# Weight scaling taken off GpSimd, small squares moved to ScalarE, and a new written-out order in a fused attention and MoE kernel

## The chip, the cores and the metric

The kernel runs on one core of one Trainium2 chip. The core has five queues of work that matter here: TensorE (PE; its weight loads are listed as PEld), VectorE (DVE), ScalarE (ACT), GpSimd (POOL), and SyncE (SP), whose queue issues all the DMAs of this kernel. The metric is the device time of one execution in microseconds; lower is better.

## The reference

Three layers follow each other over 2304 tokens (4 batches of 576), in float32:

```python
# attention: 8 heads of 64, causal window of 128, ALiBi bias
scores = where(mask, q @ k.T / sqrt(64) + bias, -1e9)
x = softmax(scores) @ v                          # -> 2304 x 512
# layer 1
h = x @ w_in                                     # 512 -> 1024
solu = h * softmax(h)
x = (layer_norm(solu) * g_ln) @ w_out            # 1024 -> 512
# layer 2
h = x @ w2_in                                    # 512 -> 2048
out = (h * sigmoid(h)) @ w2_out                  # 2048 -> 512
```

## The kernel before

**Numbers in halves.** TensorE multiplies float16. Each float32 operand is scaled by a power of two and split into a high and a low float16 half, and each product is made of three matmuls (high by high, high by low, low by high). So each weight, each attention tile and each activation costs passes on VectorE, ScalarE or GpSimd before TensorE may use it.

**The weights.** Four matrices are cut into 48 slots of 128x512 (8 of `w_in`, 8 of `w_out`, 16 each of `w2_in` and `w2_out`; the profile drops the 2, so the rows call both input matrices `in_moe_w_in_dram` and both output matrices `in_moe_w_out_dram`). They lie in memory as 64-bit numbers. A slot is loaded by SP into a `stage` tile of 512 KB (five such tiles in all), decoded into `W` by one ScalarE pass (L432) and two VectorE passes (L434 and L436, in `decode`), and its sum of squares is collected on TensorE (`gram`, L369). From the sums of a whole matrix comes its scale (`norm_scale`; the tiles `swin`, `swout`, `sw2in`, `sw2out`), and only then does `split_weight` make the halves. The string `E_W` has one letter for each slot: with "V" the high half is one scaling pass and the low half one VectorE pass that scales and subtracts (L520); with "G" the slot is scaled in place (`scaled`, L303 on ScalarE, L304 on VectorE, L306 on GpSimd), copied to float16 (L298 or L299) and subtracted (L310 on VectorE, L311 on GpSimd); with "P" the low half is made by TensorE with a diagonal matrix (L353, L354).

**The tokens.** There are 18 blocks of 128 tokens. For each, attention goes through four pairs of heads: scores into the PSUM tile `sa` (L700), a VectorE pass that adds the bias and finds the maximum (`mx`, L726), the exponential on ScalarE (L731), splitting and turning, and the product with `v` (L786). Then come layer 1's first product (L833), the layer norm, and for each two blocks (a chunk) layer 1's second product (`m1_out`, L933), whose result `y` is split (L938, L941), and layer 2 in 8 steps (L970, then L1002). `m1_out` also squares two sums twice (`shrs`, `shrr`, L915) to find the chunk's scale.

**The order.** Nothing is scheduled on the chip. The program records some 3000 operations, and the table `ORDER` lists them in the order in which they are written into the engines' queues; the strings `PICK`, `ROOT`, `NORM`, `ON_PE` and `E_W` say which engine does an operation that several could do. Each engine works through its queue in order and waits on semaphores.

Of the kernel before, what the change touches and what calls it, by code (L numbers as in the profile page):

```python
# [69 lines left out]
class Sched:  # L70
# [49 lines left out]
    def link(self, pools):  # L120
# [13 lines left out]
        for p in pools:  # L134
# [8 lines left out]
            for tag, bufs in p.tags.items():  # L143
                if any(b.free for b in bufs):
                    turn, prev = Turn(bufs[0].n), None
                    for b in bufs:
# [15 lines left out]
                for j, b in enumerate(bufs):  # L162
                    al = node()
# [13 lines left out]
                    prev = al  # L177

# [76 lines left out]
def fused_kernel(ctx, tc, qk, qn, kn, vt, rel, w_in, w_out, g_ln, w2_in, w2_out, out):  # L255
# [74 lines left out]
    gcol = Buf(const, [P, KF1], F32, "gcol")  # L330
# [3 lines left out]
    half = Buf(const, [P, 1], F32, "half")  # L334
    minus = Buf(early2, [P, P], F16, "minus")
# [23 lines left out]
    def diagonal(by):  # L359
        d = Buf(early2, [P, P], F32, "diag", 2)  # L360
# [3 lines left out]
    def gram(c, tiles, high, r, at, last, columns=False):  # L364
# [13 lines left out]
    def trace(c, acc):  # L378
        junk = Buf(early, [P, 512], BF16, "sq", 2)
        v(P + 40, lambda: V.tensor_tensor_reduce(junk[:, 0:P], c[:, 0:P], unit.tile, 1.0, 0.0, ALU.mult, ALU.add, acc.tile),  # L380
          [c, unit], [junk, acc])

    def norm_scale(name, parts, gain=None, columns=False):


        al, u, r = (Buf(const, [P, 1], F32, "nrm" + x, 2) for x in "bcd")
        whole = Buf(early2, [P, 1], F32, "nrmw", 1) if gain is not None else None
        big, scl = Buf(const, [P, 1], F32, "Q" + name), Buf(const, [P, 1], F32, "s" + name)
        if columns:
            top = Buf(const, [P, 1], F32, "nrma", 2)  # L390
# [6 lines left out]
        else:  # L397
            tot = Buf(const, [P, 1], BF16, "nrmt", 2)
# [20 lines left out]
    def decode(st, slot, j):  # L419
# [10 lines left out]
        if DECODE[j // 2] == "A":  # L430
# [3 lines left out]
            v(580, lambda: V.tensor_scalar(low(), low(), 2.0 ** -29, 7.0, ALU.mult, ALU.min), [(st, 0)],  # L434
              [(st, "low")], fast=True)
# [60 lines left out]
    def split_weight(name, slot0, n, cols, per_k=None):  # L496
        diags = {}
        for j in range(n):
            def go(j=j):
# [8 lines left out]
                if E_W[b] == "P":  # L508
# [4 lines left out]
                    scaled(("wh", b), 512, lambda: W16(b, 0), lambda: W[:, a, :], scl, [(W, a), src], [(W, b)])  # L513
# [4 lines left out]
                if E_W[b] == "V":  # L518
                    scaled(("wh", b), 512, lambda: W16(b, 0), lambda: W[:, a, :], scl, [(W, a), src], [(W, b)])
# [4 lines left out]
                scaled(("wc", b), 512, lambda: W[:, a, :], lambda: W[:, a, :], scl, [(W, a), src], [(W, a)], True)  # L524
# [4 lines left out]


# [54 lines left out]
    def v_norm(b):  # L585
# [7 lines left out]
        if on_pe:  # L593
            c = Buf(ps_early, [P, 512], F32, "gram", 2)
        else:
            s.op([("G", 150, lambda: G.memset(acc.tile, 0.0), False)], [], [acc])
        for n, i in enumerate(here):
            rows = slice(max(0, first - i * P), min(P, stop - i * P))

            def go(n=n, i=i, rows=rows):  # L600
# [7 lines left out]
                junk = Buf(early, [P, 512], BF16, "sq", 2)  # L608
# [24 lines left out]
    def v_split(i):  # L633
# [4 lines left out]
        scaled(("vh", i), 512, lambda: t[:, :, 0, :], lambda: r.tile, lambda: sv.tile, [r, sv], [(t, 0)])  # L638
        if V_SPLIT[i] == "P":
# [430 lines left out]
    n = 0  # L1070
# [278 lines left out]
```

## Time and profile before

| | us |
|---|---|
| time before, median of 3 runs (lowest to highest) | 722.03 (721.37 to 722.71) |
| time of the profiled execution | 722.29 |
| its span, from the first to the last instruction | 720.5 |
| PE busy in the span | 688.8 (96%) |
| DVE, ACT, POOL busy in the span | 428.6, 348.3, 133.8 |

Busy time is the time in which an engine executed an instruction; the rest of the span is idle time, and a wait is idle time with the instruction named that ended it. The profiled execution lies 0.26 us above the median of the three runs.

### The profile page before, as it was taken

Reading aid. Unit: us, or ns where it says so; the run is one execution under the profiler, and the core shown is the slowest. Engines: PE = TensorE matmul, PEld = TensorE weight load, DVE = VectorE, ACT = ScalarE, POOL = GpSimd, SP = SyncE. Lnnn points to the kernel's source line nnn. Section 1 sums busy time; section 2 is a strip of 40 time slices with the busy share of each in tenths; the row PEclk is TensorE's granted clock in tenths of the full one; section 3 lists DMA queues with packets and bytes.
Section 4 is the critical chain, followed back from the end, with each engine's and each line's share of the span. In section 5 each row is a group of like instructions: output and inputs, shape, how many; then the busy total and the mean of one; then the engine's idle time right before and its main releaser. Section 6 shows DMA issues by size and latency. Waiting matters only on the chain.

```text
span 720.5 us, 14218 instructions
## 1 busy us (share of the span) xinstructions
PE 688.8 (96%) x5687; PEld 473.5 (66%) x5687; DVE 428.6 (59%) x1141; ACT 348.3 (48%) x753; POOL 133.8 (19%) x132
## 2 busy tenths in 40 slices
PE   4897888999999999999999999999999999999997
PEld 2655565887555667668667765876667746788753
DVE  3899898887987547546754647678644442131120
ACT  4889877645566437425653434364423231241231
POOL 0004075213342142133121212011200100100000
PEclk9999999999999999999999999999999999999999
DMA  8888833754257353426361707264412110200000
GB/s 259 289 303 273 274 121 102 147 118 89 45 103 149 80 109 70 96 57 130 76 126 37 117 16 132 45 123 84 61 45 59 30 45 1 59 30 1 1 30 29
DMA packets 124338, 71.38 MB, mean 99 GB/s; under 512 B 108656, under 2 KB 109040, under 8 KB 124272
## 3 DMA queue, kind: packets, MB, share of 16 engines
q1 hardware_dynamic: 124272, 70.48, 40.3%
q8 instruction: 44, 0.72, 0.4%
q14 instruction: 22, 0.18, 0.1%
HBM read 39.52 MB, written 4.72 MB: 61 GB/s over the span
## 4 chain that ended last, share of the span: by engine, by line
PE 79%; DVE 12%; DMA 5%; ACT 1%; issue 1%; SPq 1%; POOL 0%; ACTq 0%; DVEq 0%
PE mm L1002 24%; PE mm L970 24%; PE mm L933 12%; PE mm L833 10%; PE sa L700 4%; DVE W L436 2%; PE mm L786 2%; DMA stage<-in_moe_w_in_dram 2%; DVE e L726 1%; DVE stage L434 1%; DMA lnT<-ln 1%; DVE W L520 1%; DMA stage<-in_moe_w_out_dram 1%; DMA vraw<-in_vt_dram 1%; PE sa L786 1%
## 5 line engine op out<-in xcount | busy, mean ns | idle before, releaser
L970 PE MATMUL mm<-y,W 128*128 128x256 f16 x1728 | 206.4, 273 | 2.4 <-DVE t L980 2.3
L1002 PE MATMUL mm<-W,g 128*128 128x512 f16 x867 | 205.9, 378 | 0.0
L970 PEld LDWEIGHTS <-W 128*128 128x128 f16 x1728 | 166.9, 98 | 38.3 <-issue 2.8
L1002 PEld LDWEIGHTS <-g 128*128 128x128 f16 x867 | 82.4, 98 | 78.4 <-issue 0.3
L933 PE MATMUL mm<-lnT,W 128*128 128x256 f16 x864 | 103.8, 273 | 0.0
L833 PE MATMUL mm<-W,xT 128*128 128x512 f16 x432 | 101.0, 383 | 0.0
L933 PEld LDWEIGHTS <-W 128*128 128x128 f16 x864 | 83.4, 98 | 16.8 <-issue 0.5
L731 ACT ACTIVATE e<-e,mx 128x256 f32<-128x256 f32 (+1 forms) x144 | 70.0, 487 | 45.5 <-DVE mx L726 44.7
L980 DVE SCALAR_TENSOR_TENSOR t<-t,mm 128x512 f32<-128x512 f32 x72 | 48.6, 681 | 60.3 <-ACT t L979 60.1
L983 DVE SCALAR_TENSOR_TENSOR g<-t,g 128x512 f16<-128x512 f32 x72 | 54.3, 756 | 50.4 <-ACT g L982 50.0
L979 ACT ACTIVATE t<-mm,cs 128x512 f32<-128x512 f32 x72 | 48.1, 678 | 62.5 <-PE mm L970 57.1
L982 ACT ACTIVATE g<-t 128x512 f16<-128x512 f32 x72 | 44.9, 625 | 67.4 <-PE mm L1002 64.9
L833 PEld LDWEIGHTS <-xT 128*128 128x128 f16 x432 | 41.6, 99 | 47.7 <-issue 3.2
L726 DVE CUSTOM_DVE_ANT_0 e<-sa,table 128x256 f32<-128x256 f32 (+1 forms) x144 | 54.4, 401 | 12.1 <-POOL a L311 4.2
L700 PE MATMUL sa<-k,q 64*128 64x128 f32 x544 | 48.2, 306 | 11.3 <-DMA q<-in_qn_dram 5.3
L700 PEld LDWEIGHTS sa<-k,q 64*128 64x128 f32 x544 | 37.3, 196 | 27.1 <-issue 10.3
L311 POOL TENSOR_TENSOR a<-e,a 128x512 f16<-128x512 f32 (+1 forms) x28 | 33.2, 1190 | 92.9 <-ACT a L298 42.3
L849 ACT ACTIVATE e<-mm,lnst,sig 128x1024 f32<-128x1024 f32 x18 | 21.6, 1200 | 54.5 <-DVE lnst L848 49.7
L311 POOL TENSOR_TENSOR ln<-e,ln 128x1024 f16<-128x1024 f32 x14 | 30.3, 2162 | 94.5 <-ACT ln L298 77.4
L847 DVE TENSOR_REDUCE lnst<-mm 128x1 f32<-128x1024 f32 x18 | 21.9, 1219 | 34.5 <-PE mm L833 34.5
L786 PEld LDWEIGHTS <-aT 128*128 128x128 f16 x816 | 32.1, 99 | 10.4 <-issue 3.3
L941 DVE SCALAR_TENSOR_TENSOR y<-mm,cs,y 128x512 f16<-128x512 f32 x18 | 13.4, 747 | 40.6 <-ACT y L938 40.6
(166 smaller groups left out, 720.7 us busy)
## 6 DMA issues: line engine op xcount, KB each, us to landing
stage<-in_moe_w_in_dram SPq DMA_DIRECT2D x24, 512.0 KB, 5.5
stage<-in_moe_w_out_dram SPq DMA_DIRECT2D x24, 512.0 KB, 4.0
k<-in_kn_dram SPq DMA_DIRECT2D x18, 256.0 KB, 3.1
vraw<-in_vt_dram SPq DMA_DIRECT2D x18, 256.0 KB, 3.6
q<-in_qn_dram SPq DMA_DIRECT2D x18, 256.0 KB, 3.6
out_dram<-t SPq DMA_DIRECT2D x17, 256.0 KB, 2.0
aT<-a SPq DMA_TRANSPOSE x56, 3.3
lnT<-ln SPq DMA_TRANSPOSE x32, 2.8
```

What stands on the lines that cost most here:

```text
L311: ("G", cg(n), lambda: G.tensor_tensor(dst(), a(), b(), op), True)], r, w, pick=pick)
L700: T.matmul(SA[:, j, off + sl * P:off + (sl + 1) * P], q[rows, p, :], k[rows, p, :], start=True, stop=sl not in blank)
L726: v(n + 20, lambda j=j: V.tensor_tensor_reduce(e[:, j, lo:lo + n], SA[:, j, off + lo:off + lo + n], table[:, 2 * p + j, o:o + n], -0.125, ...
L731: act(n, lambda j=j: A.activation(e[:, j, lo:lo + n], e[:, j, lo:lo + n], AF.Exp, bias=mx[:, j:j + 1], scale=-1.0, accum_out=rs[:, 2 * p + ...
L786: T.matmul(heads(i)[:, h // 4, h % 4, :], t[:, (2 * ha + j) * nh + c, :], vb[sl][:, h, hv, :], start=(n == 0), stop=(n == 3 * nh - 1))
L833: T.matmul(pt[:, half * 512:(half + 1) * 512], x[:, hx, k, :], W16(2 * k + half, hw), start=(k == 0 and hx + hw == 0), stop=(k == KD - 1 a ...
L933: T.matmul(pt[:, ct % 2], W16(8 + k, hw)[:, ct * P:(ct + 1) * P], l[:, hx * KF1 + k, :], start=(k == 0 and hw + hx == 0), stop=(k == KF1 - ...
L970: T.matmul(pt[:, mm], W16(16 + 4 * k + m // 4, hw)[:, (m % 4) * P:(m % 4 + 1) * P], y[:, hx, k, :], start=(k == 0 and hw + hx == 0), stop= ...
L979: act(512, lambda: A.activation(t.tile, flat(pt.tile), AF.Tanh, scale=cs[:, 0:1]), [pt, (cs, 0)], [t], extra=1)
L980: v(512, lambda: V.scalar_tensor_tensor(out=t.tile, in0=t.tile, scalar=1.0, in1=flat(pt.tile), op0=ALU.add, op1=ALU.mult), [t, pt], [t])
L983: v(512, lambda: V.scalar_tensor_tensor(out=flat(g[:, 1]), in0=t.tile, scalar=2.0 ** -16, in1=flat(g[:, 0]), op0=ALU.mult, op1=ALU.subtrac ...
L1002: T.matmul(pt[:, cols], g[:, hg, mm, b * P:(b + 1) * P], W16(32 + m, hw)[:, cols], start=(m == 0 and hg + hw == 0), stop=(m == KF2 - 1 and ...
```

## The change

1. Weight slots are no longer scaled by GpSimd: the alternative is taken out of `scaled` for the slots (`GC` is False; `GH`, for the high halves, is new and False too). The 16 passes go to VectorE and ScalarE.
2. The two squares in `m1_out` are made by ScalarE's Square, not by VectorE.
3. Slot 1 of `w_in` goes from TensorE ("P") to "G", one slot of `w2_out` from "V" to "G". Attention tiles of block 2 and the x tile of block 0 take their low half by a VectorE subtraction ("P" in `ON_PE`), not by a TensorE matmul with `minus` and a copy ("Q").
4. `ORDER` and the engine strings are found anew. Over the whole program ScalarE gets 34 more instructions, VectorE 20 fewer, GpSimd 17 fewer, PE 13 fewer. Five of GpSimd's 14 subtractions for the layer norm's halves (`ln`) go to VectorE.
5. Other lines of the diff (`GRAM`, the letter "R" of `DECODE`, `needs`, `late`, `free=True`, a memset of `under`) are switched off, or only state when a buffer may be given out while the order is checked; they add no pass. The numbers in `load` and `transpose` are planning costs that leave no trace in the program.

```diff
-                scaled(("wc", b), 512, lambda: W[:, a, :], lambda: W[:, a, :], scl, [(W, a), src], [(W, a)], True)
+                scaled(("wc", b), 512, lambda: W[:, a, :], lambda: W[:, a, :], scl, [(W, a), src], [(W, a)], GC)
...
         for src, dst in ((sh, s4), (s4, s8r)):
-            v(60, lambda src=src, dst=dst: V.tensor_tensor(dst.tile, src.tile, src.tile, ALU.mult), [src], [dst])
+            s.op([("A", 130, lambda src=src, dst=dst: A.activation(dst.tile, src.tile, AF.Square), False)], [src], [dst])
...
-ORDER = [8, 21, 9, 7, 1685, 0, 1, 6, 4, 1665, 39, 10, 22, 24, 23, 25, 11, 14, 13, 17, 15, 50, 12, 2, 40, 266,
+ORDER = [10, 1675, 6, 7, 1, 11, 22, 4, 9, 23, 40, 24, 25, 26, 51, 41, 21, 15, 18, 45, 55, 267, 266, 192, 17,
...
-E_W = "PPPPPPPPGVVGVVGGVGGVVGGVGVGGGGGVGVGGGGGVGVVGGGGG"
+E_W = "PGPPPPPPGVVGVVGGVGGVVGGVGVGGGGGVGGGGGGGVGVVGGGGG"
...
-ROOT = "GGGGVVGGGGGGGVVVGG"
-NORM = "VAAAGGGAGGAVGAVGGV"
-ON_PE = {"a": "QQQQDDDDDDDDDDDDDD", "x": "QQQQDDDDDDDDDDDDDD", "l": "QQDDDDDDDDDDDDDDDD"}
...
+ROOT = "GGGGVGGGGGGGGVVVGG"
+NORM = "GAAAGGGAGAAVGAVGGV"
+ON_PE = {"a": "QQPQDDDDDDDDDDDDDD", "x": "PQQQDDDDDDDDDDDDDD", "l": "QQDDDDDDDDDDDDDDDD"}
...
+GH = False
+GC = False
```

Three places show what the new table does. The first is VectorE, after the scale `sw2in` of the third matrix is known, between the two maxima of block 4's second pair of heads (`L726 ISA e,mx` before, `L759 ISA e,mx` with the change; TensorE's scores of the third pair wait for the second of them). Of before these are the last twelve of the 21 rows from the one maximum to the other:

```order
L875 TENSOR_SCALAR lnst<-lnst 128x1
L436 SCALAR_TENSOR_TENSOR W<-stage 128x512
L304 TENSOR_SCALAR W<-W,sw2in 128x512
L520 SCALAR_TENSOR_TENSOR W<-W,sw2in 128x512
L941 SCALAR_TENSOR_TENSOR y_122<-mm,cs,y_122 128x512
L299 CAST a_101<-e 128x512
L304 TENSOR_SCALAR W<-W,sw2in 128x512
L520 SCALAR_TENSOR_TENSOR W<-W,sw2in 128x512
L434 TENSOR_SCALAR stage<-stage 128x512
L654 SCALAR_TENSOR_TENSOR vs<-vraw,sv_103,vs 128x8x64
L1047 TENSOR_SCALAR q_186<-Qwout,Qw2in 128x1
L726 ISA e,mx<-sa,table 128x256
```

With the change these are all the rows from the one maximum to the other:

```order
L759 ISA e,mx<-sa,table 128x256
L759 ISA mx 128x1
L424 TENSOR_SCALAR Qw2in<-nrmc 128x1
L313 TENSOR_SCALAR W<-W,sw2in 128x512
L884 TENSOR_SCALAR lnst<-lnst,sig_156 128x1
L886 RECIPROCAL lnst<-lnst 128x1
L612 COPY sv_100<-sv_103 64x1
L830 RECIPROCAL rinv<-rinv 128x8
L655 TENSOR_SCALAR sig_102<-sig_102 128x1
L887 SCALAR_TENSOR_TENSOR e_1289,lnst<-e_1289,lnst,mm_1201 128x1024
L890 TENSOR_SCALAR lnst<-lnst 128x1
L759 ISA e,mx<-sa,table 128x256
```

Before, 16 passes of 128x512 and a few small ones stood between the two maxima; now it is one of 128x512 and one of 128x1024.

The second place is GpSimd's queue in the same part of the program, between the layer norm of block 1 (`lnst`) and the subtraction for the attention tiles of block 4 (`a`). Before, with the passes on `sw2in` (L306):

```order
L306 TENSOR_SCALAR W<-W,sw2in 128x512 x5
L311 TENSOR_TENSOR W<-W 128x512 x2
L306 TENSOR_SCALAR W<-W,sw2in 128x512 x2
L311 TENSOR_TENSOR W<-W 128x512
L861 TENSOR_SCALAR lnst<-lnst 128x1
L863 TENSOR_TENSOR lnst<-lnst,half 128x1
L311 TENSOR_TENSOR W<-W 128x512 x3
L311 TENSOR_TENSOR a_101<-e,a_101 128x512
L311 TENSOR_TENSOR ln_104<-e_1344,ln_104 128x1024
L306 TENSOR_SCALAR W<-W,sw2in 128x512
L311 TENSOR_TENSOR W<-W 128x512 x3
```

With the change:

```order
L320 TENSOR_TENSOR W<-W 128x512
L1059 MEMSET blank_rows 1x128 x2
L320 TENSOR_TENSOR W<-W 128x512 x3
L320 TENSOR_TENSOR a_98<-e,a_98 128x512
L894 TENSOR_SCALAR lnst<-lnst 128x1
L896 TENSOR_TENSOR lnst<-lnst,half 128x1
L320 TENSOR_TENSOR W<-W 128x512 x3
L320 TENSOR_TENSOR a_99<-e,a_99 128x512
L320 TENSOR_TENSOR W<-W 128x512 x4
```

The scaling passes are gone, the subtraction of the layer norm's halves (`ln`, 128x1024) that stood here has left the queue at this place, and the subtractions on `W` (L311 before, L320 now) have stayed.

The third place is the queue of SP, where the last loads of `w2_in` stand beside the loads of `v` for blocks 5 to 8 (`vraw`). Before:

```order
L473 DMA stage<-in_moe_w_in_dram 128x1024 x12
L664 DMA q<-in_qn_dram 128x512
L663 DMA k<-in_kn_dram 128x512
L473 DMA stage<-in_moe_w_in_dram 128x1024 x4
L473 DMA stage<-in_moe_w_out_dram 128x1024
L631 DMA vraw<-in_vt_dram 128x512 x2
L473 DMA stage<-in_moe_w_out_dram 128x1024
L631 DMA vraw<-in_vt_dram 128x512 x2
L473 DMA stage<-in_moe_w_out_dram 128x1024 x3
```

With the change:

```order
L494 DMA stage<-in_moe_w_in_dram 128x1024 x10
L697 DMA q<-in_qn_dram 128x512
L696 DMA k<-in_kn_dram 128x512
L663 DMA vraw<-in_vt_dram 128x512
L494 DMA stage<-in_moe_w_in_dram 128x1024 x2
L663 DMA vraw<-in_vt_dram 128x512 x2
L494 DMA stage<-in_moe_w_in_dram 128x1024 x2
L663 DMA vraw<-in_vt_dram 128x512
L494 DMA stage<-in_moe_w_in_dram 128x1024 x2
L697 DMA q<-in_qn_dram 128x512
L494 DMA stage<-in_moe_w_out_dram 128x1024 x4
```

The four `vraw` loads, which stood after the last load of `w2_in`, now stand before it.

## Rows read from the trace of the kernel before

**Rows 1.** The profile's page: the span, and its part 1.

```profile
span 720.5 us, 14218 instructions
PE 688.8 (96%) x5687; PEld 473.5 (66%) x5687; DVE 428.6 (59%) x1141; ACT 348.3 (48%) x753; POOL 133.8 (19%) x132
```

**Rows 2.** Stretches: length; PE, PEld, DVE, ACT, POOL busy; PEclk; DMA share; GB/s.

```profile
0.00:20.00 20.00, 10.48 (x61) 6.87 (x61) 7.55 (x36) 10.16 (x31) 1.57 (x13) 1.00 0.83 263
20.00:60.00 40.00, 36.18 (x305) 22.91 (x303) 36.22 (x116) 34.85 (x82) 5.24 (x6) 1.00 0.85 297
60.00:90.00 30.00, 23.42 (x242) 16.34 (x243) 26.28 (x73) 26.51 (x56) 3.62 (x7) 0.94 0.80 267
90.00:120.00 30.00, 24.68 (x226) 18.14 (x225) 29.62 (x75) 22.71 (x44) 19.95 (x18) 0.98 0.27 86
120.00:200.00 80.00, 78.22 (x718) 59.05 (x717) 65.70 (x151) 46.07 (x95) 23.18 (x21) 0.99 0.48 108
```

**Rows 3.** PE's waits, 0 to 90 us: total, times, longest.

```profile
PE gram L369 <- DVE W L436: 3.7, 4, 2.5
```

**Rows 4.** PE's waits, 90 to 125 us, and PE's timeline there.

```profile
PE sa L700 <- DVE mx L726: 4.0, 2, 3.5
118.13 0.49 PE L700 MATMUL sa<-k,q 64*128 64x128 f32 x4 [3.48 <-DVE mx L726]
```

**Rows 5.** Timeline of DVE, 104 to 119 us: start, duration.

```profile
104.61 0.48 DVE L304 TENSOR_SCALAR W<-W,sw2in 128x512 f16<-128x512 f32 x1
105.12 0.75 DVE L520 SCALAR_TENSOR_TENSOR W<-W,sw2in 128x512 f16<-128x512 f32 x1
...
108.22 1.38 DVE L304 TENSOR_SCALAR W<-W,sw2in 128x512 f16<-128x512 f32 x1
...
111.29 1.39 DVE L304 TENSOR_SCALAR W<-W,sw2in 128x512 f16<-128x512 f32 x1
112.72 1.52 DVE L520 SCALAR_TENSOR_TENSOR W<-W,sw2in 128x512 f16<-128x512 f32 x1
114.17 2.35 DVE L434 TENSOR_SCALAR stage<-stage 128x512 uint32<-128x512 uint32 x1
...
117.66 0.41 DVE L726 CUSTOM_DVE_ANT_0 e<-sa,table 128x256 f32<-128x256 f32 x1
...
118.60 0.41 DVE L434 TENSOR_SCALAR stage<-stage 128x512 uint32<-128x512 uint32 x1
```

**Rows 6.** Timeline of POOL in the same stretch.

```profile
106.59 2.72 POOL L311 TENSOR_TENSOR W<-W 128x512 f16<-128x512 f32 x2
111.13 1.27 POOL L311 TENSOR_TENSOR W<-W 128x512 f16<-128x512 f32 x1 [1.81 <-ACT W L298]
112.36 1.33 POOL L311 TENSOR_TENSOR a<-e,a 128x512 f16<-128x512 f32 x1
113.66 2.57 POOL L311 TENSOR_TENSOR ln<-e,ln 128x1024 f16<-128x1024 f32 x1
116.22 0.86 POOL L306 TENSOR_SCALAR W<-W,sw2in 128x512 f32<-128x512 f32 x1
```

**Rows 7.** Groups of instructions by shape: count, busy, mean ns.

```profile
L306 POOL TENSOR_SCALAR W<-W,sw2in 128x512 f32<-128x512 f32 x8 | 7.0, 884 | 0.8 <-DVE lnst L875 0.8
...
L353 PE MATMUL mm<-W,diag 128*128 128x512 f32 x16 | 8.5, 615 | 0.0
...
L303 ACT ACTIVATE W<-W,gs 128x512 f16<-128x512 f32 x4 | 2.8, 712 | 0.0
...
L561 PE MATMUL mm<-aT,minus 128*128 128x512 f16 x12 | 4.5, 379 | 0.7 <-ACT aT L557 0.6
...
L915 DVE TENSOR_TENSOR shrr<-shrs 128x2 bf16<-128x2 f32 x9 | 4.5, 500 | 0.1
...
L731 ACT ACTIVATE e<-e,mx 128x128 f32<-128x128 f32 x16 | 6.3, 394 | 3.2 <-DVE mx L726 2.4 <-DVE Qv L414 0.7
```

**Rows 8.** The chain that ended last: start, duration, what.

```profile
70.48 7.34 DMA stage<-in_moe_w_out_dram
```

More of the change, by code (lines that the diff above doesn't have):

```diff
@@ L177, in link @@
                     prev = al
+        for p in pools:
+            for b in p.bufs:
+                for x in b.needs:
+                    self._edge(x.alloc, b.alloc)
+                for o in b.late:
+                    self._edge(o, b.alloc)
     def solve(self):
@@ L369, in go @@
                 T.matmul(c[:, o:o + P], high(x), high(x), start=(at + x == 0), stop=(at + x == last))
-        pe(68 * tiles, go, r, [c])
+        pe(66 * tiles, go, r, [c])
     def column_max(c, acc, f):
-        junk = Buf(early, [P, 512], BF16, "sq", 2)
+        junk = Buf(early, [P, 512], BF16, "sq", 2, free=True)
         v(552, lambda: V.tensor_tensor_reduce(junk.tile.rearrange("p (a b) -> p a b", a=4), c.tile.rearrange("p (a b) -> p a b", a=4),
@@ L462, in load_weight @@
         nf = cols // 512
-        acc = Buf(const, [P, nf if columns else 1], F32, "acc" + name)
+        by_squares = [] if columns else [j for j in range(n) if GRAM[slot0 + j] == "A"]
+        by_gram = [j for j in range(n) if j not in by_squares]
+        acc = Buf(const, [P, nf if columns else 1 + len(by_squares)], F32, "acc" + name)
+        if not by_gram:
+            s.op([("G", 150, lambda: G.memset(acc[:, 0:1], 0.0), False)], [], [(acc, 0)])
         view = w.bitcast(U32).rearrange("(k p) (f e) -> p k f e", p=P, f=nf)
@@ L478, in go @@
             def go(at, k, sl):
-                size = n // nf if columns else n
-                if at % size == 0:
-                    sums[name] = Buf(ps_early, [P, 512], F32, "gram", 2)
+                if at in by_squares:
+                    junk = Buf(early, [P, 512], BF16, "sq", 2, free=True)
+                    c = 1 + by_squares.index(at)
+                    act(590, lambda: A.activation(junk.tile, W[:, sl, :], AF.Square, accum_out=acc[:, c:c + 1]),
+                        [(W, sl)], [junk, (acc, c)], extra=2)
+                    return
+                size = n // nf if columns else len(by_gram)
+                z = by_gram.index(at)
+                if z % size == 0:
+                    sums[name] = Buf(ps_early, [P, 512], F32, "gram", 2, free=True)
                 def high(x):
@@ L528, in split_weight, with made @@
             go()
+    def made(slots):
+        return [s.state[W][b][0] for b in slots if any(E_W[x] == "P" for x in slots)]
     def make_table():
@@ L547, in turned_parts @@
         tp = Buf(ps, [P, 2, 2 * P], F32, "mm", 2, free=True)
+        tp.needs = [x[0] for x in w[:1]]
         def bank():
@@ L593, in v_norm @@
         if on_pe:
[L594 removed]
+            c = Buf(ps_early, [P, 512], F32, "gram", 2, free=True)
         else:
@@ L642, in v_split @@
             by.src = sv
-            d = diagonal(by)
+            d = diagonal(by, "vdiag", 1)
             pt = Buf(ps, [P, 512], F32, "mm", 2, free=True)
+            pt.needs = [t]
             def go():
@@ L927, in m1_out @@
             pt = Buf(ps, [P, 2, 2 * P], F32, "mm", 2)
+            pt.late = made(range(8, 16))
             for ct in (c0, c0 + 1):
@@ L963, in m2_in @@
         pt = Buf(ps, [P, 2, 2 * P], F32, "mm", 2)
+        pt.late = made({16 + 4 * k + (2 * j + x) // 4 for k in range(KD) for x in range(2)})
         for mm in range(2):
```

73 lines of the change are left out of this document (42 added, 31 removed), and 332 rows, old and new, of the table ORDER.

## The prediction

> **What bounds the kernel now.** The reading starts with the page's part 1: TensorE is busy for 688.8 us of a span of 720.5 [rows 1]. The time is therefore TensorE's work and 31.7 us in which it waits, and a change can only act on those two. The second view is the table of stretches, which says where the waits lie. TensorE is idle for 9.5 us of the first 20, 3.8 us from 20 to 60, 6.6 us from 60 to 90, 5.3 us from 90 to 120 and 1.8 us from 120 to 200 [rows 2]; the other 4.7 us lie later, most of them behind the last matmuls. After 120 us there is always a matmul ready, so the question is how early TensorE gets into that state.
>
> The third view is who else is full while TensorE waits. From 20 to 60 us VectorE is busy for 36.2 of 40 us and the DMA engines for 0.85 of the time. From 90 to 120 us it is VectorE alone: 29.6 of 30 us, beside 22.7 on ScalarE and a DMA share of 0.27. That is also where GpSimd works most, 19.95 of 30 us [rows 2].
>
> The fourth view is the list of TensorE's waits from 90 us on. Its largest entry is 4.0 us for a maximum on VectorE, and 3.48 us of it is one wait, of the scores of block 4's third pair, which start at 118.13 [rows 4]. VectorE's timeline shows why that maximum came only at 117.66. Four passes ahead of it in its queue are long: two scalings (L304) take 1.38 and 1.39 us where one outside this place takes 0.48, one L520 takes 1.52 instead of 0.75, and one L434 takes 2.35 instead of 0.41 [rows 5]. That is 0.90 + 0.91 + 0.77 + 1.94 = 4.5 us. Beside each of them GpSimd is in a long pass, and each ends a little after that pass does: the L434 that starts at 114.17 ends at 116.52, GpSimd's subtraction for the layer norm at 113.66 + 2.57 = 116.23; the L304 from 111.29 ends at 112.68, GpSimd's pass at 112.40 [rows 5, 6]. A VectorE pass that meets such a GpSimd pass waits for its end and then runs.
>
> **The change, part by part.**
>
> *TensorE's work.* One slot no longer needs its low half from TensorE: two matmuls with the diagonal at 8.5 / 16 = 0.53 us and one with `minus`, taken at the 4.5 / 12 = 0.38 us of the attention tiles [rows 7], 1.4 us. Five more matmuls with `minus` go, 1.9 us. That is 3.3 us at most. They stand in the early blocks, ahead of the 6.6 us of waits between 60 and 90 us, where the time can turn into waiting; so the least is 0. I take a third, 1.1 us.
>
> *The wait at 118 us.* In the new order 16 passes of 128x512 no longer stand between the two maxima of block 4's second pair: one of that size and one of 128x1024 do. GpSimd's 16 scaling passes are gone, 8 of them on `sw2in` with 0.88 us each [rows 7], and so is its 2.57 us subtraction, beside which the longest VectorE pass lay [rows 6]. Against that, GpSimd's subtractions on `W` (L311) remain in this stretch, and VectorE has more to do between the scale `sw2in` and the second half of the first `y`: three more scalings of `sw2in` and one of `gs` at 0.48 us, and more decoding brought forward, about 2 us in all. So the next thing late is `y` itself. Of the 5.3 us of waits in this stretch the bounds are 0 and 5.3 given back. I take 3.0: the 4.5 us of stretched passes and 0.5 us for squares that leave VectorE here, less 2 us of added passes. This is nearer to the upper bound because the maximum that TensorE waited for is moved ahead by far more than the wait was long.
>
> *60 to 90 us.* TensorE waits here for decoded slots: 3.7 us in four waits, the longest 2.5 us [rows 3]. The chain shows what this one hangs on: a load of `w2_out` that was issued at 70.48 and took 7.34 us [rows 8], beside four `vraw` loads; its decoding stood in VectorE's queue ahead of a slot that TensorE wanted. In the new SP queue all loads of `w2_in` are issued before the next of `w2_out`, so that wait should shrink, by at most its 2.5 us. But the four `vraw` loads (128 x 512 x 4 bytes, 0.26 MB each) now stand ahead of the last `w2_in` loads: 1.05 MB at the 267 GB/s of this stretch [rows 2] would be 3.9 us. TensorE needs those `v` tiles before the scale in both orders, so I expect little of this to show. Bounds: 2.5 us won, 3.9 us lost; taken: 1.0 us won.
>
> *ScalarE.* It gets 34 instructions more. Thirteen are scalings at 0.71 us [rows 7], 9 us over the first 200 us. It has 7.3 us free from 90 to 120 and 34 us from 120 to 200 [rows 2], so I cost them at nothing; in the first 90 us the decoding competes with them, and some 2.3 us more stand ahead of the first gate. That is the price if the cover is missing. The 18 squares have no row on ScalarE; the nearest is an activation of 128x128 with 0.39 us [rows 7], which includes 128 columns that a square of two columns does not have. So each costs between nothing and 0.39 us, 7 us in all at most, over the whole run. Each leaves VectorE, where the mean of the second was 0.50 us [rows 7]. They are on the way to `y`, but a step earlier than the wait that decides.
>
> *The sum.* It is made against the profiled execution, 722.3 us (its span and 1.8 us around it), 0.3 us above the median of the runs: 722.3 - 1.1 - 3.0 - 1.0 = **717.2 us**.
>
> **The rivals.**
>
> *The lock stays.* GpSimd's subtractions on `W` and on the attention tiles remain, and three of the four long passes lay beside one of these [rows 5, 6]; with VectorE's 2 us more, the waits of 90 to 120 us would come back in front of `y`, as long as before. Only the removed matmuls would count: 722.3 - 1.1 = 721.2 us, no change that can be told. Speaking for it is that L436, L520 and L654, which read two tiles from SBUF, are as many as before; against it, that no maximum is queued behind them any more. It decides if VectorE's stretched passes in this stretch still add up to more than about 4 us.
>
> The Trainium skill bears on this one: "SBUF — State Buffer", section "Who interferes with whom", says that VectorE and GpSimd share a pair of ports that is locked for a whole instruction, and that a VectorE instruction with two SBUF inputs contends with any GpSimd instruction that reads SBUF, not only fast copies and scalings. By that rule taking scalings off GpSimd leaves the subtractions as blockers, which speaks against the change and gives this rival's 721.2 us, where the row of the 2.35 us pass beside a subtraction that left the queue gives the forecast's 717.2. The trace agrees that an L520, which has two SBUF inputs, was held: 1.52 us against 0.75 [rows 5].
>
> *The loads decide (slower).* If the last `w2_in` slots land 3.9 us later, the scale `sw2in` comes that much later, everything on VectorE behind it too, and the removed matmuls become waiting: 722.3 + 3.9 = 726.2 us if none of the stretched time comes back, 723.2 with the 3.0 us. It is slower than before as soon as the delay is larger than what is given back behind it. For it speaks a DMA share of 0.80 in 60 to 90 us [rows 2]; against it, that the bytes needed before the scale are nearly the same.
>
> *More than expected.* All 5.3 and 2.5 us and the 3.3 us of matmuls: 711.2 us.
>
> **How the numbers follow.** Less than 0.2% (1.4 us) either way can hardly be told from no change. The forecast gets 0.67, the lock 0.18, the loads 0.12, more than expected 0.03. Faster by over 0.2% (below 720.6): the first and the last, and 0.03 of the lock, together 0.73. Within 0.2%: the rest of the lock and 0.01 of the loads, 0.16. Slower: 0.11. The likeliest case alone spans 714 to 720. The range for 8 in 10 reaches from 712.5, near the sum of the upper bounds, to 722.8, which holds the lock's case and leaves out most of the loads'.
>
> **What would show it.** In the profile after, TensorE's busy time falls to 686 or 687 us. From 90 to 120 us TensorE is idle for under 3 us, no scores wait more than 1 us for a maximum, and no L451 or L313 (the old L434 and L304) there takes over 2 us. From 60 to 90 us no wait for a decoded slot exceeds 1.5 us. From 200 us on nothing changes. The forecast is wrong if TensorE's first matmuls on `y` wait for VectorE for 3 us or more, or if the waits before 90 us grow.

## The result, and the profile after

The changed kernel takes 714.58 us (median of 6 runs, 713.60 to 716.90) against 721.70 us: a ratio of 0.9909, with an interval of 0.9892 to 0.9926, or 7.1 us less. The forecast was 717.2 us, with 714 to 720 for the likeliest case. The profiled execution takes 714.52 us, 7.8 us less than that of before.

First the page, then the table of stretches, in the columns of [rows 1] and [rows 2]:

```profile
span 712.7 us, 14216 instructions
...
PE 682.6 (96%) x5679; PEld 472.3 (66%) x5679; DVE 423.9 (59%) x1121; ACT 360.7 (51%) x787; POOL 111.3 (16%) x115
```

```profile
0.00:20.00 20.00, 10.71 (x71) 7.66 (x71) 9.40 (x40) 12.54 (x35) 1.26 (x10) 1.00 0.86 300
20.00:60.00 40.00, 32.74 (x289) 20.79 (x287) 35.15 (x111) 33.11 (x76) 3.89 (x4) 1.00 0.85 284
60.00:90.00 30.00, 23.73 (x216) 16.69 (x216) 27.08 (x72) 26.92 (x56) 4.70 (x9) 0.94 0.66 224
90.00:120.00 30.00, 27.75 (x277) 20.71 (x276) 29.77 (x85) 26.38 (x57) 13.44 (x13) 1.00 0.45 144
120.00:200.00 80.00, 79.94 (x736) 59.54 (x733) 64.74 (x160) 53.48 (x112) 29.78 (x22) 1.00 0.47 106
```

TensorE's busy time fell by 6.2 us (688.8 to 682.6) and its idle time by only 1.6 (31.7 to 30.1). By stretch the idle time went from 9.5 to 9.3, from 3.8 to 7.3 (20 to 60 us), from 6.6 to 6.3, from 5.3 to 2.25 (90 to 120 us) and from 1.8 to 0.1. The waits from 90 to 120 us are less, those from 20 to 60 us more.

TensorE's waits after, from 90 to 200 us, in the columns of [rows 4]; no scores wait for a maximum any more:

```profile
PE gram L379 <- DVE W L453: 0.8, 1, 0.8
PE mm L354 <- DVE nrmt L412: 0.6, 1, 0.6
PE mm L593 <- DVE mx L759: 0.5, 1, 0.5
PE sa L733 <- DVE xm L832: 0.3, 1, 0.3
```

What came in from 20 to 60 us lies mostly behind 55 us: a wait of 1.48 us for a VectorE tile (`xm`), and one of 2.60 us, which ends at 60.90, for block 3's k, whose load stands behind the last scores of the block before. TensorE's timeline (start, duration, what, and in brackets the wait), and the table of stretches behind it:

```profile
56.90 0.71 PE L733 MATMUL sa<-k,q 64*128 64x128 f32 x8 [1.48 <-DVE xm L832]
57.55 0.41 PE L379 MATMUL gram<-W 128*128 128x128 bf16 x4
57.79 0.51 PE L819 MATMUL sa<-vs,aT 128*128 128x64 f16 x12
60.90 1.23 PE L733 MATMUL sa<-k,q 64*128 64x128 f32 x8 [2.60 <-DMA k<-in_kn_dram]
```

```profile
58.00:60.00 2.00, 0.30 (x11) 0.18 (x7) 1.55 (x7) 0.01 (x1) 0.85 (x1) 1.00 0.78 277
60.00:62.00 2.00, 1.10 (x8) 0.96 (x8) 2.00 (x4) 2.00 (x5) 0.00 (x0) 0.71 0.64 178
62.00:64.00 2.00, 2.00 (x12) 1.88 (x11) 1.92 (x7) 2.00 (x6) 0.00 (x0) 0.50 1.00 367
64.00:66.00 2.00, 1.45 (x26) 1.14 (x23) 0.62 (x4) 0.93 (x4) 0.00 (x0) 0.94 0.87 322
```

Behind the wait the granted clock falls to its lower level, 0.50 or 1.2 GHz. Matmuls are longer there: the eight score matmuls at 60.90 take 1.23 us, the eight at 56.90, at 2.4 GHz, 0.71 us.

The same length shows that the clock column does not tell the start of an execution. It gives 1.00 for the first 20 us, yet eight score matmuls take 1.23 us there too:

```profile
18.98 1.23 PE L733 MATMUL sa<-k,q 64*128 64x128 f32 x8
24.70 0.72 PE L733 MATMUL sa<-k,q 64*128 64x128 f32 x8
```

In minus_back (below) the column gives 0.50 for the same matmuls at 18.99 us, and they take the same 1.23 us. So up to about 23 us most matmuls run at the lower level whether the column says so or not, and clocks of the first 20 us cannot be compared between kernels.

VectorE's long passes after, in the columns of [rows 5], and GpSimd beside them:

```profile
103.56 1.20 DVE L313 TENSOR_SCALAR W<-W,sw2in 128x512 f32<-128x512 f32 x1
...
111.98 1.52 DVE L687 SCALAR_TENSOR_TENSOR vs<-vraw,sv,vs 128x512 f16<-128x512 f32 x1
113.42 1.37 DVE L313 TENSOR_SCALAR W<-W,sw2in 128x512 f16<-128x512 f32 x1
114.71 1.65 DVE L453 SCALAR_TENSOR_TENSOR W<-stage 128x512 uint32<-128x512 uint32 x1
```

```profile
103.31 1.17 POOL L320 TENSOR_TENSOR W<-W 128x512 f16<-128x512 f32 x1 [3.42 <-DVE W L308]
...
110.22 4.29 POOL L320 TENSOR_TENSOR W<-W 128x512 f16<-128x512 f32 x3
114.47 1.34 POOL L320 TENSOR_TENSOR a<-e,a 128x512 f16<-128x512 f32 x1
```

Outside this place an L687 takes 0.74 us and an L453 0.70 (means from 30 to 90 us), and a scaling takes the 0.48 of [rows 5]. The excess of these four is 0.72 + 0.78 + 0.89 + 0.95 = 3.3 us, where it was 4.5.

The view that settled most splits the span at TensorE's first matmul on `y`, which starts at 123.82 us before and at 119.42 after. Before, then after:

```profile
0.00:123.82 123.82, 98.58 (x840) 65.71 (x841) 103.33 (x305) 96.08 (x214) 31.15 (x44) 0.97 0.69 232
123.82:720.50 596.68, 590.23 (x4848) 407.79 (x4846) 325.28 (x836) 252.26 (x540) 102.68 (x89) 1.00 0.35 72
```

```profile
0.00:119.42 119.42, 94.36 (x843) 65.32 (x844) 100.81 (x305) 98.37 (x220) 23.14 (x35) 0.99 0.71 238
119.42:712.70 593.28, 588.26 (x4837) 406.93 (x4835) 323.05 (x817) 262.29 (x568) 88.12 (x81) 1.00 0.35 72
```

Of the 7.8 us, 4.4 are won up to `y` and 3.4 behind it. The two orders do not put the same work on either side of `y`: eight matmuls are gone, yet three more stand ahead of it and eleven fewer behind. Up to `y` TensorE is idle for 25.2 us before and 25.1 after. VectorE, however, is busy for 2.5 us less (103.33 to 100.81) and idle for 1.9 us less (20.5 to 18.6), and 1.85 us of that lies in the first 20 us. Behind `y` TensorE has 2.0 us less to do (11 fewer matmuls recorded) and waits 1.4 us less.

The clock is not what makes most of the gain. At one mean clock, 0.997, two executions of the changed kernel took 713.6 and 714.2 us, and eighteen of the kernel before, run beside the experiments below, 720.8 on average.

### The profile page after: what moved, and what is told of

Same layout as the page of the kernel before. It is cut to its first block, busy times and chain, and to the rows that moved or that the text cites. A ratio compares the mean times of both kernels' runs of the same rounds, so it can differ in the third digit from the quotient of the medians.

```text
span 712.7 us, 14216 instructions
## 1 busy us (share of the span) xinstructions
PE 682.6 (96%) x5679; PEld 472.3 (66%) x5679; DVE 423.9 (59%) x1121; ACT 360.7 (51%) x787; POOL 111.3 (16%) x115
## 4 chain that ended last, share of the span: by engine, by line
PE 84%; DVE 7%; DMA 4%; ACT 2%; issue 1%; SPq 0%; POOL 0%; ACTq 0%; DVEq 0%
PE mm L1005 26%; PE mm L1037 25%; PE mm L967 13%; PE mm L866 11%; PE sa L733 5%; PE mm L819 2%; DMA stage<-in_moe_w_in_dram 2%; DVE W L453 1%; PE sa L819 1%; DVE stage L451 1%; DMA k<-in_kn_dram 1%; DMA lnT<-ln 1%; PE gram L379 1%; DVE e L759 1%; DMA aT<-a 1%
## 5 line engine op out<-in xcount | busy, mean ns | idle before, releaser
L1037 PE MATMUL mm<-W,g 128*128 128x512 f16 x867 | 208.0, 378 | 0.0
L967 PEld LDWEIGHTS <-W 128*128 128x128 f16 x864 | 83.3, 98 | 16.8 <-issue 0.8
L759 DVE CUSTOM_DVE_ANT_0 e<-sa,table 128x256 f32<-128x256 f32 (+1 forms) x144 | 54.4, 402 | 17.0 <-PE sa L733 7.3
L320 POOL TENSOR_TENSOR a<-e,a 128x512 f16<-128x512 f32 (+1 forms) x25 | 30.0, 1201 | 87.8 <-ACT a L307 52.8
L320 POOL TENSOR_TENSOR W<-W 128x512 f16<-128x512 f32 x21 | 27.4, 1309 | 76.7 <-DVE W L308 48.6
```

Source lines behind the costliest of these rows:

```text
L320: ("G", cg(n), lambda: G.tensor_tensor(dst(), a(), b(), op), True)], r, w, pick=pick)
L759: v(n + 20, lambda j=j: V.tensor_tensor_reduce(e[:, j, lo:lo + n], SA[:, j, off + lo:off + lo + n], table[:, 2 * p + j, o:o + n], -0.125, ...
L967: T.matmul(pt[:, ct % 2], W16(8 + k, hw)[:, ct * P:(ct + 1) * P], l[:, hx * KF1 + k, :], start=(k == 0 and hw + hx == 0), stop=(k == KF1 - ...
L1037: T.matmul(pt[:, cols], g[:, hg, mm, b * P:(b + 1) * P], W16(32 + m, hw)[:, cols], start=(m == 0 and hg + hw == 0), stop=(m == KF2 - 1 and ...
```

## The experiments

All are compared with the kernel before. The table splits each profiled execution at its first matmul on `y`, as above; the idle times are the stretch less the busy time.

| kernel | ratio (interval) | `y` at | VectorE busy / idle to `y` | TensorE idle to / after `y` | clock to `y` |
|---|---|---|---|---|---|
| before | 1 | 123.8 | 103.3 / 20.5 | 25.2 / 6.4 | 0.97 |
| changed | 0.9909 (0.9892 to 0.9926) | 119.4 | 100.8 / 18.6 | 25.1 / 5.0 | 0.99 |
| max_early | 0.9995 (0.9977 to 1.0012) | 118.9 | 99.4 / 19.5 | 20.4 / 10.1 | 0.99 |
| old_order_no_pool_scaling | 1.0001 (0.9983 to 1.0020) | 121.8 | 103.2 / 18.6 | 21.9 / 6.8 | 0.99 |
| new_program_old_order | 1.0034 (1.0021 to 1.0047) | 122.1 | 100.7 / 21.4 | 23.8 / 8.5 | 0.96 |
| old_program_new_order | 1.0139 (1.0116 to 1.0162) | 127.3 | 100.4 / 26.9 | 26.8 / 10.2 | 0.91 |
| no_diag | 0.9985 (0.9973 to 0.9997) | 124.1 | 103.5 / 20.6 | 28.3 / 6.1 | 0.96 |
| diag_twice | 0.9964 (0.9948 to 0.9980) | 123.7 | 101.1 / 22.7 | 23.5 / 4.3 | 0.99 |
| minus_back | 0.9948 (0.9926 to 0.9969) | 124.5 | 99.2 / 25.4 | 26.6 / 4.8 | 0.90 |
| v_twice | 1.0012 (0.9996 to 1.0027) | 121.4 | 102.6 / 18.8 | 25.1 / 9.4 | 0.96 |
| pool_scaling_back | 0.9966 (0.9945 to 0.9988) | 122.7 | 103.4 / 19.3 | 25.3 / 4.5 | 0.94 |
| pool_scaling_back_filled | 0.9914 (0.9898 to 0.9930) | 121.6 | 104.2 / 17.4 | 25.4 / 4.2 | 1.00 |
| k_second | 0.9916 (0.9891 to 0.9942) | 118.8 | 101.0 / 17.8 | 24.2 / 4.8 | 0.99 |
| k_second_filled | 0.9887 (0.9871 to 0.9902) | 117.9 | 101.1 / 16.8 | 20.5 / 5.5 | 0.99 |

**max_early.** The kernel before; one operation is moved.

```diff
-820, 1053, 500, 478, 470
+820, 1053, 1054, 500, 478, 470
...
-879, 1054, 1661, 552
+879, 1661, 552
```

> The kernel before, with one operation moved in its order: the second maximum of block 4's second pair stands right behind the first, no longer behind 16 passes of VectorE. Nothing else changes; GpSimd keeps its scalings and its subtractions. Theory (the place of the maximum in the queue is what cost): the 3.48 us wait of the third pair's scores falls under 1 us, TensorE's granted clock does not fall between 118 and 124 us, and the time falls by 2 to 5 us, a ratio to before of 0.993 to 0.997. Rival (the wait comes back in front of y or of another pass, since VectorE has as much to do and is held as often): ratio 0.999 to 1.001, with a new wait of 2 us or more between 100 and 125 us.

The wait at 118 us is gone and `y` starts 4.9 us earlier, but the time is the same: the theory fell. TensorE's waits from 90 to 140 us show where the wait went:

```profile
PE mm L970 <- DVE t L980: 2.6, 1, 2.6
PE mm L554 <- DVE shra L918: 0.9, 1, 0.9
PE mm L970 <- POOL W L311: 0.8, 1, 0.8
```

The 16 passes that the maximum jumped are needed a little later, ahead of the first gates (L980). TensorE reaches `y` with less of VectorE's work done, and waits 10.1 us behind it instead of 6.4. A later point shows the same. TensorE's first matmul on `g`, the gates' result, starts at nearly the same time before and in max_early:

```profile
176.54 2.75 PE L1002 MATMUL mm<-W,g 128*128 128x512 f16 x12
176.16 2.75 PE L1002 MATMUL mm<-W,g 128*128 128x512 f16 x12
```

Of the 4.9 us at `y` 0.4 are left there. So a start of `y` is worth something only with VectorE's work done up to it. A second theory took the first one's place: the whole of VectorE's work up to the gates sets the time.

**old_order_no_pool_scaling.** The kernel before; the engine letters of the 16 slots that GpSimd scaled are those of the changed kernel (eleven to ScalarE and five to VectorE, not ten and six).

```diff
-"wc": "AVGAAAAAGAAGAAGGAGGGAGGAGAVGAGGAAGAGAGVAVVAVAGGV"
+"wc": "AVGAAAAAAAAVAAAAAVVGAVAAAAVAAAAAAGAAAAVAVVAVAAVV"
```

> The kernel before in its own order, with GpSimd's 16 scalings of weight slots given to ScalarE (10) and VectorE (6) as the changed kernel has them. Theory: the second maximum of block 4's second pair stays behind its passes, of which there are now more on VectorE, and GpSimd's subtractions still hold VectorE; TensorE still waits 2 us or more for that maximum, and the ratio to before is 0.998 to 1.005. Rival (taking the scalings off GpSimd is what gains, by less contention): VectorE's passes there fall to their undisturbed times, the wait is under 1 us and the ratio is 0.990 to 0.995.

As the theory had it: no gain, and TensorE's waits from 90 us on begin with the same maximum:

```profile
PE sa L700 <- DVE mx L726: 3.1, 1, 3.1
```

**new_program_old_order** and **old_program_new_order.** No line is changed but the list: each kernel's operations in the other's order, as far as dependencies and free tiles allow. In the first 24 operations stand elsewhere than in the order that was to be copied, in the second 140, so the second is only roughly the changed kernel's order.

> The changed kernel's instructions (its table of engines, no scalings on GpSimd, squares on ScalarE, eight TensorE matmuls fewer), put into the order of the kernel before as far as dependencies and free tiles allow; 24 of some 3000 operations stand otherwise than there. Theory (the order gains: neither a single maximum moved nor the scalings off GpSimd gained alone, so it is the whole queue of VectorE up to the first gates at about 135 us): ratio to before 0.996 to 1.002, TensorE's waits before 140 us as long as before. Rival (the instructions gain: TensorE's removed matmuls, and less on GpSimd): ratio 0.990 to 0.995.

> The other half: the instructions of the kernel before, with all its matmuls and GpSimd's 16 scalings, put into the order of the changed kernel; 140 operations stand otherwise than there, since a tile was not yet free. Theory (the order gains): ratio to before 0.991 to 0.996, with y reached 3 us or more earlier. Rival (the instructions gain): 0.997 to 1.003. If both halves give about half, 0.995, the gain is shared.

Both are slower than either kernel, which none of the expectations had. In these runs order and instructions gain only together: each list fits its own set. In the old program with the new order VectorE is idle for 26.9 us up to `y`, and TensorE's clock is low in each of the first three stretches:

```profile
0.00:20.00 20.00, 10.01 (x71) 7.13 (x71) 9.51 (x40) 12.73 (x35) 1.51 (x11) 0.86 0.87 301
20.00:60.00 40.00, 35.89 (x270) 22.53 (x268) 31.48 (x103) 30.58 (x70) 4.14 (x3) 0.86 0.80 268
60.00:90.00 30.00, 22.93 (x216) 16.80 (x217) 24.20 (x68) 23.78 (x53) 3.73 (x6) 0.89 0.68 222
```

On busy time alone the clock loses 35.89 x 0.14 + 22.93 x 0.11 = 7.5 us in the second and third, against 1.4 in the changed kernel; part of the 7.5 lies before 24 us, where the changed kernel's matmuls are as long. How much of the slowness is the clock's and how much the 140 operations' stays open. The new program in the old order has 2.4 us more TensorE work behind `y` than the changed kernel (590.6 against 588.3 us), as the kernel before has: so that work moves with the order.

**no_diag.** The kernel before.

```diff
-            if diag is not None:
-                T.matmul(pt[:, 0:n], diag.tile, whole(), start=True, stop=False)
-            T.matmul(pt[:, 0:n], minus.tile, high(), start=False, stop=True)
+            T.matmul(pt[:, 0:n], minus.tile, high(), start=True, stop=True)
```

> The kernel before without the matmuls of its eight w_in slots with the diagonal; the low halves of these slots then lack their main part, and nothing is added on another engine. TensorE's busy time falls by the 8.5 us of that row. Theory (work of TensorE in the first 60 us is paid for the most part, as the doubled matmuls showed: 4.0 us for 5.7): 5 to 7 us faster, ratio to before 0.990 to 0.993. Rival (my prediction: two thirds of it turn into waits before 90 us): ratio 0.995 to 0.997.

The matmuls of that row, 8.5 us, bring 0.15%, 1.1 us. The two parts of its span:

```profile
0.00:124.10 124.10, 95.85 (x825) 64.90 (x826) 103.53 (x305) 96.82 (x217) 32.19 (x45) 0.96 0.70 232
124.10:720.40 596.30, 590.17 (x4848) 407.81 (x4846) 328.05 (x836) 251.69 (x537) 101.71 (x88) 1.00 0.34 71
```

VectorE has the same work and `y` comes at the same time. Up to `y` TensorE's busy time falls by only 2.7 us (98.6 to 95.9), and its idle time rises by 3.0: what is left out turns into waits. A part is the clock: it falls to 0.50 from 55 to 58 us, behind waits of 1.09 and 0.78 us that the kernel before does not have, and summed over stretches of 1 us up to `y` it loses 4.5 us of busy time, against 3.4 before. The rest of the difference between 8.5 and 2.7 us is not accounted for. The theory that this work is paid fell for the old order; even my third was too much.

**diag_twice.** The changed kernel.

```diff
+                T.matmul(pt[:, 0:n], diag.tile, whole(), start=True, stop=True)
                 T.matmul(pt[:, 0:n], diag.tile, whole(), start=True, stop=False)
```

> The changed kernel with each matmul of a weight slot with the diagonal (seven slots of w_in, between 30 and 55 us) done twice into the same bank; the first result is overwritten by the second. By the timeline of the changed kernel two such matmuls in a row take 1.02 to 1.07 us and one 0.59, so seven more are 3.3 to 6 us of TensorE's time by how they overlap. Theory (work added to or taken from TensorE in the first 60 us is paid in full, since what follows is a chain through TensorE): the time grows by as much as TensorE's busy time does, 3 to 6 us, ratio to before 0.995 to 0.999. Rival (my prediction: two thirds of it are hidden in waits): busy time grows by as much but the waits of the first 60 us shrink, the time grows by 1 to 2 us, ratio 0.992 to 0.994.

Busy time is 5.7 us more (688.3), the time 0.9964 - 0.9909 = 0.0055 or 4.0 us. Here VectorE is idle for 22.7 us up to `y` instead of 18.6: it waits for TensorE. So work added at 30 to 55 us is mostly paid in the new order, and work taken away in the old one is not. That is no contradiction if VectorE bounds both and TensorE stands just behind it; the opposite pair, leaving work out in the new order and adding it in the old one, was not tried.

**minus_back.** The changed kernel.

```diff
-ON_PE = {"a": "QQPQDDDDDDDDDDDDDD", "x": "PQQQDDDDDDDDDDDDDD", "l": "QQDDDDDDDDDDDDDDDD"}
+ON_PE = {"a": "QQQQDDDDDDDDDDDDDD", "x": "QQQQDDDDDDDDDDDDDD", "l": "QQDDDDDDDDDDDDDDDD"}
```

> The changed kernel with five matmuls with the matrix minus given back to TensorE (block 2's attention tiles and block 0's x), as the kernel before has them; the five subtractions from PSUM leave VectorE and five evictions go to ScalarE. Theory (TensorE's work is paid nearly in full): busy time grows by 1.9 us, the time by 1 to 2 us, ratio to before 0.992 to 0.994. Rival (VectorE is what bounds the first 130 us, and gets back five passes of 0.6 to 0.7 us): the time falls or stays, ratio 0.988 to 0.991.

It is 2.8 us slower than the changed kernel's ratio, more than either expected. The profile cannot give this to the matmuls: the clock was 0.90 and 0.83 from 20 to 60 and from 60 to 90 us, where the changed kernel has 1.00 and 0.94. (The 0.87 of the first 20 us costs nothing: the score matmuls at 18.99 us are as long as the changed kernel's.) Of its seven executions three took 715.4 to 715.6 us and four 717.4 to 719.4. Inconclusive.

**v_twice.** The changed kernel.

```diff
+                    def low():
+                        for _ in range(2 if 16 <= b < 32 else 1):
+                            V.scalar_tensor_tensor(out=W16(b, 1), in0=W[:, a, :], scalar=scl(), in1=W16(b, 0),
+                                                   op0=ALU.mult, op1=ALU.subtract)
```

> The changed kernel with the subtraction of six w2_in slots on VectorE (L548, 0.75 us, between 90 and 130 us) done twice, into the same place: 4.5 us more on VectorE where it is busy for 29.8 of 30 us. Theory (from 90 us to the gates VectorE bounds as much as TensorE's own work does): the time grows by 2.5 to 4.5 us, ratio to before 0.9945 to 0.997, and TensorE waits for VectorE between 110 and 140 us. Rival (with the maximum ahead of the long passes VectorE has slack there): it grows by less than 1 us, ratio 0.990 to 0.9925.

The time grows by 1.0012 - 0.9909 = 0.0103, 7.4 us. VectorE's busy time grew by more than the 4.5 us planned, by 7.1 us on the page (431.0), and all of it is paid: VectorE is the bound here. The clock cannot be the reason, though it was at 0.50 from 61 to 70 us: VectorE's first doubled subtraction starts at 101.92 us, 0.36 later than in the changed kernel (101.56), and TensorE's first matmul on `g` at 172.71, 8.1 us later than there (164.59), which is all that the two profiled executions differ by. The two parts of its span, and TensorE's waits from 110 to 160 us:

```profile
0.00:121.40 121.40, 96.32 (x843) 66.99 (x844) 102.62 (x306) 98.04 (x220) 22.41 (x35) 0.96 0.69 231
121.40:720.80 599.40, 590.02 (x4837) 407.81 (x4835) 328.36 (x822) 263.14 (x568) 88.52 (x81) 1.00 0.34 72
```

```profile
PE mm L1008 <- DVE t L1018: 3.0, 2, 2.3
PE mm L1008 <- DVE y L978: 1.3, 1, 1.3
PE mm L589 <- DVE y L978: 0.6, 1, 0.6
```

**pool_scaling_back** and **pool_scaling_back_filled.** The changed kernel with the letter "G" again for those 16 slots; then the same with idle matmuls, whose two operations stand in the list right ahead of the last scores of block 2 and the first of block 3.

```diff
+    for n in (11, 9,):
+        f = Buf(ps, [P, 512], F32, "mm", 2, free=True)
+        def fill(f=f, n=n):
+            for _ in range(n):
+                T.matmul(f[:, 0:3 * P], ones.tile, table[:, 0, :], start=True, stop=True)
+        pe(160 * n, fill, [ones, (table, 0)], [f])
```

> The changed kernel in its new order, with the same 16 scalings of weight slots given back to GpSimd. Theory: VectorE's passes are held more often, but no maximum that TensorE wants soon is queued behind them; the ratio to before is 0.990 to 0.995, near the changed kernel's 0.991, with TensorE idle for under 4 us from 90 to 120 us. Rival (GpSimd's scalings are the cost): the gain of the waits is lost, ratio 0.996 or more, and TensorE waits 3 us or more longer between 90 and 125 us.

> The changed kernel with the 16 scalings back on GpSimd, and 20 matmuls of 128x384 whose results nobody reads, put on TensorE where that kernel waited 2.4 and 1.6 us (at 55 and 59 us), ahead of the scores. There its granted clock fell to 0.50 from 58 to 71 us. Theory (what the scalings on GpSimd cost is the clock behind these waits): the clock stays at 1.00 between 58 and 72 us and the time falls from 0.9966 to 0.990 to 0.993 of before, although TensorE has 3.2 us more work. Rival (it is contention itself, and the clock is only an effect): 0.996 or more.

The scalings cost 4.1 us (0.9966 against 0.9909), and 20 matmuls that do nothing take 3.8 us of it back. The stretches from 54 to 74 us without and with them:

```profile
54.00:58.00 4.00, 1.59 (x15) 1.06 (x13) 3.32 (x4) 2.31 (x6) 1.82 (x2) 1.00 0.78 289
58.00:62.00 4.00, 2.36 (x26) 2.06 (x24) 2.58 (x9) 1.04 (x1) 0.38 (x1) 0.51 0.53 146
62.00:66.00 4.00, 3.34 (x25) 3.14 (x24) 2.88 (x8) 3.81 (x12) 0.00 (x0) 0.50 0.87 286
66.00:70.00 4.00, 2.99 (x28) 2.23 (x26) 3.17 (x12) 2.64 (x5) 1.11 (x3) 0.50 0.28 106
70.00:74.00 4.00, 4.00 (x30) 2.66 (x29) 4.00 (x9) 3.38 (x8) 3.47 (x4) 0.79 0.83 281
```

```profile
54.00:58.00 4.00, 3.38 (x25) 2.09 (x25) 3.59 (x4) 2.59 (x6) 1.81 (x2) 1.00 0.79 310
58.00:62.00 4.00, 3.22 (x41) 2.10 (x37) 2.81 (x9) 1.27 (x3) 0.66 (x1) 1.00 0.49 148
62.00:66.00 4.00, 2.49 (x34) 2.03 (x33) 3.81 (x14) 4.00 (x12) 0.00 (x0) 1.00 0.91 326
```

The first kernel came out as its rival had it (0.996 or more), the second as its theory had it. So a large part of what GpSimd's scalings cost here is the clock: the two executions without filling that had a mean clock of 0.997 took 714.8 and 715.8 us, the filled kernel 715.7. How large stays open. The two profiled executions differ by 1.6 us (717.31 and 715.74), not by 3.8, so other executions must have lost more than this trace shows; and with the clock kept `y` is still 2.2 us later than in the changed kernel. k_second_filled (below), which is filled in the same places and has no such scalings, is 1.9 us faster than this filled kernel (0.9887 against 0.9914).

**k_second** and **k_second_filled.** The changed kernel with block 0's k loaded second; then with 7 and 12 idle matmuls in the same two places.

```diff
-ORDER = [10, 1675, 6, 7, 1, 11, 22, 4, 9, 23, 40
+ORDER = [10, 9, 1675, 6, 7, 1, 11, 22, 4, 23, 40
```

> The changed kernel with block 0's k loaded second instead of fourth. TensorE's first scores start at about 5.3 us, as before, not at 7.0. Theory (a wait at the start is hidden, since VectorE and the loads bound the first 60 us): other waits grow by as much, ratio to before 0.990 to 0.992, like the changed kernel. Rival (every wait of TensorE is paid): 1.6 us faster, ratio 0.9887 or less.

> The changed kernel with block 0's k loaded second (0.9916 without the rest) and 19 such idle matmuls where it waits 1.5 and 2.6 us, at 55 and 58 us. Theory (the fall of the clock from 60 to 64 us costs 1.5 us): the clock stays at 1.00 there, ratio to before 0.988 to 0.990, faster than both kernels. Rival (the filled waits delay the scores by as much): ratio 0.991 to 0.993.

The first scores start at 4.4 us instead of 7.0, and the time stays: that wait is hidden. With the filling the clock stays at 1.00 from 54 to 66 us, but it falls behind the next wait (1.94 us, at 75 us) to 0.58 and 0.56. Both came out as their theories had it. The ratio is the lowest measured; its interval overlaps that of the changed kernel.

## Why the prediction came out, point by point

**What bounds.** TensorE's work and waits are the right account, but what sets the waits up to the gates is VectorE's work as a whole (v_twice, max_early), not one late maximum. TensorE's idle time to `y` hardly moved, though eight matmuls were gone.

**TensorE's work (-1.1, bounds 0 to -3.3).** Mis-sized against the page: busy time fell by 6.2 us, outside the bounds. The removed matmuls are about 3.2 us by their rows, and the clock loses 2.0 us less of busy time (3.4 before, 1.4 after: busy time x (1 - granted clock), summed over stretches of 2 us up to the 96th matmul on `y`). The last 1.0 us has no cause shown. Less busy time is no gain by itself: no_diag took out 8.5 us and got 1.1. What the time shows is the 2.0 us less work behind `y`; that the removed matmuls made room for it is argued, not shown.

**The wait at 118 us (-3.0, bounds 0 to -5.3).** The size was right: waits from 90 to 120 us fell from 5.32 to 2.25 us. That it was is in part luck, since the working has a right and a wrong half. VectorE's balance, 4.5 + 0.5 - 2 = 3.0 us, compares with the 2.5 us that VectorE is busy less up to `y`, though the stretched passes gave back only 4.5 - 3.3 = 1.2 us of it (the prediction's 4.5 leaves out a fifth long pass, the L654 at 116.44 with 1.17 us, which is the L687 counted above; like for like it is 4.9 against 3.3). The step that failed is the reason for choosing near the upper bound, that the maximum is "moved ahead by far more than the wait was long": max_early moves just that, in the old order, and gains nothing.

**60 to 90 us (-1.0).** Measured -0.3. The waits for decoded slots in the first 90 us went from 3.7 us to 0.9, as said, and the wait for k took their place. The stretch from 20 to 60 us, with 3.4 us more waiting, has no term in the sum: the announced sign of a wrong forecast, waits that grow ahead of 90 us, did come.

**Behind 120 us.** No term either; 1.7 us of waits went there, where VectorE no longer lags at the gates.

**ScalarE (0).** It is busy for 12.4 us more, and the longest wait put down to it in the first 90 us is 1.2 us, as before. The squares alone were not tried.

**The lock as a rival.** It was to decide if the stretched passes still added up to more than about 4 us. They add up to 3.3. GpSimd's subtractions do go on holding VectorE. The Trainium skill, "SBUF — State Buffer", section "Who interferes with whom", says that a VectorE instruction with two SBUF inputs contends with a GpSimd instruction that reads SBUF; the trace agrees, with an L453, which reads two halves of `stage`, of 1.65 us beside a subtraction and 0.70 elsewhere. The time that this rival gave, 721.2, did not come.

**The loads as a rival.** No wait of TensorE is put down to `vraw` or to a load of w2_in; the load that it waited for was k. VectorE's 1.85 us more work in the first 20 us (7.55 to 9.40) cannot be given to the new order of the loads: no_diag, which has the list and the instructions of the kernel before up to 30 us, has 8.84 there, and new_program_old_order 9.32.

So the sum was 2.6 us short of the median. In TensorE's balance of the two profiled executions (7.8 us, where the sum had 5.1) the busy time gave 5.1 us more than its term and 60 to 90 us 0.7 less than its own; without a term stand +3.4 us of waits from 20 to 60, -1.7 from 120 to 200, -0.2 in the first 20 and +0.3 behind 200. The total came out near the forecast because these largely cancel, which is luck and not the working. What part of the change lowers VectorE's work up to the gates was not tried apart: neither the order nor the instructions gained alone.

## What to carry to other kernels

When one wait ends last, ask whether the engine behind it is full over the whole stretch: if so, moving the awaited instruction only moves the wait, and the number to predict is when that engine has all its work done up to the next point at which TensorE never waits again (here the gates; up to `y` was not far enough, as max_early shows). Doubling an engine's work and leaving some out test which engine bounds; one of the two alone would have misled here. Each of the two orders, tuned for one set of instructions, was worth nothing to the other set, so options and order are to be judged together.

## What the runs showed of the hardware

The clock was the surprise. Each fall to 0.50 looked at here stands behind a wait, or two in a row: of 2.60 us at 60 us in the changed kernel, of 3.48 us before [rows 4] (0.50 from 119 to 122 us), of 2.4 and 1.6 us in pool_scaling_back, of 1.94 us in k_second_filled, of 1.09 and 0.78 us in no_diag. Not every wait has one behind it: the 1.48 us at 55 us in the changed kernel has none. The start of an execution is no exception, though the column gives 1.00 there: behind the changed kernel's longest wait, 7.0 us, eight score matmuls take 1.23 us.

What a fall costs is not what the busy time says. In pool_scaling_back 8.7 us of busy time from 58 to 70 us ran at about half speed, yet its profiled execution is 1.6 us longer than that of the filled kernel; in v_twice a fall from 61 to 70 us left VectorE 0.36 us late at 102 us. Over executions it shows all the same: the 12 of pool_scaling_back have mean clocks of 0.983 to 0.997; the two at 0.983 took 720.1 and 721.6 us, the two at 0.997 714.8 and 715.8. Matmuls whose results nobody reads kept the clock at 1.00 and were worth 3.8 us between the medians. The Trainium skill, "TensorE: Matmul & The Clock Gate", section "Part 1: The HAM clock gate (the "warmup" mystery)", says that the low clock is the default and activity lifts it; the traces agree, with 1.00 where the waits were filled and 0.50 where they were not. And taking away TensorE's work and adding to it were not opposites, each in its own order: leaving out 8.5 us of matmuls brought 1.1 us, doubling 7 us of them cost 4.0.
